# Bias attention and a gated feed-forward on one core: early operations merged, weight conversions moved behind unit 8, a block's last output ahead of a feed-forward step

## Chip, cores, metric

One core of a Trainium2 chip runs the whole program. The metric is the device time of one execution in microseconds. The kernel before took 741.07 us (median of 3 runs, 740.38 to 741.28).

## What is computed

```python
# q, k, v: (4 batches, 8 heads, 576 positions, 64)
scores = scale * np.matmul(q, k.transpose(0, 1, 3, 2))
x = (psi_rel / psi_i)[..., None]          # logs of distances and positions
h = np.maximum(x @ w1 + b1, 0.0)          # 32 hidden values for each pair of positions
bias = h @ w2                             # one value per head, the same for all batches
attn = softmax(scores + bias)
x = np.matmul(attn, v)                    # rows: 2304 tokens of 512
h = x @ w_in                              # 512 -> 2048
out = (h * sigmoid(1.702 * h)) @ w_out    # 2048 -> 512
```

The inputs of the feed-forward part come as 64-bit floats, all others as 32-bit. The softmax is written in the reference with its maximum and its sum.

## The kernel before, in words

**Units.** Attention is cut into 72 units of (batch b, chunk c of 128 query positions, pair of heads hp); a last chunk has 64 positions, and its units take two pairs. Two batches form a group of 36 units. Unit u issues its scores on PE (`emit_s`, L352), then its softmax (`emit_soft1`, L368): DVE adds the bias tile to the scores and finds the extreme (L378, mx), ACT takes the exponential (L385) and sums into sm, ACT or DVE makes an fp16 high part (L392, L390), POOL the low part (hl, L393), and a transposing DMA on SP's queue makes aT (L399). The output of a unit (`emit_av`) follows two units later, three in the first eight: DVE finishes sm (L414) and takes its reciprocal, PE multiplies aT with v16 (L423, L430), DVE writes xn in two fp16 parts (L436, L442). After the last pair of heads SP transposes xn into xT (L452).

**Blocks.** Two batches' outputs of one chunk form a block of 256 tokens (128 for the short chunk). Block 0 is made of units 0 to 7, block 1 of units 8 to 15, and so on. Each block has 16 feed-forward steps. A step's first half (`emit_m1`, L511) is 12 products with xT (L522), tanh on ACT (L528, th), a product on DVE (L530) and two fp16 parts, gT, on DVE or ACT and on POOL (L537, L538). Its second half (`emit_m2`, L541) comes two steps later: PE adds to the block's output in PSUM (L551, tiles op). Behind the 16th step `store` evicts (L561).

**Weights.** Every number of w_in and w_out is a 64-bit float. 32 loads of 512 KB on SP (L467) bring them in, up to three ahead, and `split_w` (L471) converts each: three unpacking instructions on DVE (L486, L489, L492), the high part on ACT (L498), the low part on DVE (`lo_part`, L224). `W_STEPS` (L86) says how many conversions unit u issues; the first half of step f needs the first 8 * (f // 4) + 4 of them.

**Bias.** 36 bias steps make the hidden values on DVE or ACT (L165, L167), multiply on PE (L188, L190), evict on ACT (L195) and store (L196). The first 8 stand before unit 0, the others with units 0 to 28. Steps 1 to 19 use the two PSUM tiles that the feed-forward outputs use later (om and ol).

**Keys and values.** `trans_k`, `trans_k_own` (L273, L286) and `split_v` (L329) transpose the keys on PE and split keys and values into fp16 high (ACT: L282, L296, L305, L344) and low parts (DVE or POOL: L224, L222), one pair of heads at a time.

**Order.** The unit loop (L683) issues, for each unit: scores and softmax, one feed-forward step (if a block is ready), the due outputs, conversions, bias work, another feed-forward step, loads. Each engine then gets a list order from a scheduler that moves instructions by its own estimates, so the lists that the engines run differ somewhat from the order of the source.

Of the kernel before, what the change touches and what calls it, by code (L numbers as in the profile page):

```python
# [20 lines left out]
def kernel(  # L21
# [26 lines left out]
    nc = tc.nc  # L48
# [17 lines left out]

    BUFS = {"st": 4, "ht": 2, "os": 2, "bt": 2, "a32": 2, "hl": 2, "aT": 2, "xT": 2, "w32": 3, "qT": 3, "kT": 8,
            "v16": 8, "gT": 3, "xn": 2}

# [15 lines left out]
    STEPS_B = {}  # L85
    W_STEPS = [1, 2, 2, 3, 3, 3, 3, 3, 3, 3, 3, 3]  # L86

# [4 lines left out]
    ps_h = ctx.enter_context(tc.tile_pool(name="ps_h", bufs=2, space=PSUM))  # L92
    ps_o = ctx.enter_context(tc.tile_pool(name="ps_o", bufs=2, space=PSUM))

# [190 lines left out]

    def trans_k_own(b, e):  # L286

        t = k_st[b, e]
        tails = ps_h.tile([128, 512], F32, tag="h", name="kt")
        ds = []  # L290
        for u in range(2):
            nc.tensor.transpose(tails[:, ST * u:ST * u + ST], kt_st[b][:, 2 * e + u, :], idn[:ST, :ST])
        for u in range(2):
            ds.append(stage([128, 2, S], F16, "kT", "kT"))
            kT[b, 2 * e + u] = ds[u]
            nc.scalar.activation(  # L296
                out=ds[u][:, 0, SM:S], in_=tails[:, ST * u:ST * u + ST], func=ACTF.Copy, scale=KS
            )
        for u in range(2):
            lo_part(False, ds[u][:, 1, SM:S], tails[:, ST * u:ST * u + ST], KS, ds[u][:, 0, SM:S])  # L300
# [28 lines left out]
    def split_v(b, e):  # L329

        src = v_st.pop((b, e)).rearrange("p u c d -> p u (c d)")
        gp = (b, e) in POOL_V
        vs = scaled(gp, src, VS)
        for u in range(2):
            d = stage([128, 2, 640], F16, "v16", "v16")
            nc.gpsimd.memset(d[0:64, :, 320:384], 0.0)
            nc.gpsimd.memset(d[64:128, :, 256:320], 0.0)
            sv, dv = src[:, u], [d[:, x] for x in range(2)]
            parts = [(sv[0:64, 256:320], *(y[0:64, 256:320] for y in dv)),
                     (sv[64:128, 256:320], *(y[64:128, 320:384] for y in dv))]  # L340
            for (x, y) in ((0, 0), (320, 384)):
                parts.append((sv[:, x:x + 256], *(z[:, y:y + 256] for z in dv)))
            for (s_, dh, dl) in parts:
                nc.scalar.activation(out=dh, in_=s_, func=ACTF.Copy, scale=vs)  # L344
                lo_part(gp, dl, s_, vs, dh)
            v16[b, 2 * e + u] = d

# [261 lines left out]
    for g in range(B // 2):  # L609
# [73 lines left out]
    for u in range(NU + 2):  # L683
# [77 lines left out]
```

## Time and profile before

| | |
|---|---|
| runs | 741.07 us median, 740.38 to 741.28 |
| profiled execution | 739.43 us; 737.7 us from first to last instruction |
| PE | 642.0 us busy, 87% |
| DVE | 482.9 us busy, 65% |
| ACT | 406.4 us busy, 55% |
| POOL | 312.2 us busy, 42% |
| granted TensorE clock, mean | 0.955 |
| chain of waits | PE 55%, DMA 18%, DVE 13%, ACT 7% |

PE is busy 9 tenths or more of most slices from 180 us on and 5 to 7 tenths before; DVE and ACT have it the other way round, and the DMA engines are near their full share up to about 180 us. The shares are means over both parts, so the views have to be cut by stage.

### The profile page before, as it was taken

What the parts mean: (1) busy time and instruction counts of PE and PEld (TensorE: products, weight loads), DVE (VectorE), ACT (ScalarE), POOL (GpSimd) and SP (SyncE); (2) the same over time, 40 slices, a digit from 0 to 9 for tenths busy, and PEclk for the clock granted to TensorE, in tenths of its full rate; (3) what the DMA queues carried; (4) which work ended last, traced back from release to release, by engine and by line L of the source; (5) the groups of instructions that cost most, each with busy time, mean ns of one, the idle gap of its engine ahead of it and who ended that gap; (6) DMA issues with size and microseconds to landing.
All of it is one profiled execution on the core that took longest, in us unless ns stands there. A gap on an engine that the chain in (4) does not pass through costs nothing.

```text
span 737.7 us, 17303 instructions
## 1 busy us (share of the span) xinstructions
PE 642.0 (87%) x6648; PEld 400.5 (54%) x6648; DVE 482.9 (65%) x1378; ACT 406.4 (55%) x905; POOL 312.2 (42%) x360
## 2 busy tenths in 40 slices
PE   6767567577989998799979889889989999999997
PEld 3223333344645664566747456566656666667764
DVE  5689698999657766446667676454774777574321
ACT  6899987477457656445445436643443444342133
POOL 2314433246434445444442555643463456453222
PEclk9986798899999999999998999999999999999999
DMA  9799999979767657958576796982794487664000
GB/s 236 231 287 261 236 250 287 273 203 215 177 118 182 157 109 162 170 121 157 129 167 127 146 173 141 183 164 52 130 174 105 97 153 163 111 113 100 9 30 16
DMA packets 249843, 116.50 MB, mean 158 GB/s; under 512 B 229792, under 2 KB 234016, under 8 KB 249760
## 3 DMA queue, kind: packets, MB, share of 16 engines
q1 hardware_dynamic: 241664, 99.38, 65.3%
q10 hardware_dynamic: 7952, 15.43, 6.3%
q8 instruction: 52, 0.85, 0.5%
q0 software_dynamic: 144, 0.59, 0.2%
q14 instruction: 31, 0.25, 0.1%
HBM read 52.85 MB, written 15.34 MB: 92 GB/s over the span
## 4 chain that ended last, share of the span: by engine, by line
PE 55%; DMA 18%; DVE 13%; ACT 7%; issue 4%; POOL 1%; SPq 0%; ACTq 0%; DVEq 0%; POOLq 0%
PE hp L522 21%; PE op L551 19%; DMA aT<-hl 13%; PE ot L430 6%; PE sp L362 4%; DVE a L378 3%; ACT a L385 3%; PE ot L423 2%; DVE w L489 2%; DVE w L492 2%; DMA w<-in_moe_w_in_dram 1%; ACT ht L165 1%; POOL hl L393 1%; PE o L188 1%; DVE w L486 1%
## 5 line engine op out<-in xcount | busy, mean ns | idle before, releaser
L393 POOL TENSOR_TENSOR hl<-a,hl 128x576 f16<-128x576 f32 x142 | 187.8, 1336 | 171.7 <-ACT hl L392 93.2
L522 PE MATMUL hp<-xT,wi 128*128 128x256 f16 (+1 forms) x1920 | 219.1, 265 | 22.4 <-DMA xT<-xn 9.2
L551 PE MATMUL op<-wo,gT 128*128 128x512 f16 x864 | 214.9, 381 | 4.1 <-DVE gT L537 2.6
L522 PEld LDWEIGHTS <-wi 128*128 128x128 f16 x1920 | 169.9, 99 | 65.3 <-issue 29.8
L538 POOL TENSOR_TENSOR gT<-th,gT 128x256 f16<-128x256 f32 (+1 forms) x160 | 106.7, 668 | 206.2 <-DVE gT L537 114.7
L528 ACT ACTIVATE th<-hp 128x256 f32<-128x256 f32 (+1 forms) x160 | 57.2, 359 | 188.7 <-PE hp L522 181.5
L385 ACT ACTIVATE a<-a,mx 128x576 f32<-128x576 f32 x144 | 110.3, 768 | 61.7 <-DVE mx L382 61.4
L530 DVE SCALAR_TENSOR_TENSOR th<-th,hp 128x256 f32<-128x256 f32 (+1 forms) x160 | 62.3, 390 | 105.7 <-ACT th L528 104.7
L378 DVE CUSTOM_DVE_ANT_0 a<-sp,bt 128x576 f32<-128x576 f32 x144 | 102.9, 751 | 29.1 <-PE sp L362 27.9
L551 PEld LDWEIGHTS <-gT 128*128 128x128 f16 x864 | 79.5, 98 | 75.8 <-issue 3.5
L165 ACT ACTIVATE ht<-tab,pk 128x576 f32<-128x576 f32 x96 | 78.6, 866 | 4.2 <-PE ol L190 4.0
L362 PE MATMUL sp<-kT,qT 64*128 64x512 f16 (+2 forms) x960 | 73.1, 296 | 7.3 <-DVE mx L378 6.0
L430 PE MATMUL ot<-v,aT 128*128 128x64 f16 (+1 forms) x1920 | 78.3, 199 | 0.0
L430 PEld LDWEIGHTS <-aT 128*128 128x128 f16 (+1 forms) x1920 | 71.3, 105 | 5.2 <-issue 4.2
L392 ACT CAST hl<-a 128x576 f16<-128x576 f32 x103 | 66.1, 665 | 8.0 <-DMA aT<-hl 7.8
L362 PEld LDWEIGHTS <-qT 64*128 64x128 f16 (+1 forms) x960 | 29.3, 99 | 53.1 <-issue 21.5
L188 PE MATMUL om<-ht,pk 128*32 128x512 f32 x152 | 44.5, 718 | 8.5 <-ACT os L195 8.4
L423 PE MATMUL ot<-v,aT 128*128 128x128 f16 (+1 forms) x240 | 29.2, 231 | 23.2 <-DMA aT<-hl 18.2
L414 DVE TENSOR_SCALAR sm<-sm 128x2 f32<-128x2 f32 x72 | 28.7, 399 | 25.9 <-ACT a L385 25.7
L537 DVE CAST gT<-th 128x256 f16<-128x256 f32 x112 | 42.5, 380 | 4.0
L167 DVE TENSOR_SCALAR ht<-tab,pk,b1n 128x576 f32<-128x576 f32 x48 | 34.4, 763 | 7.8 <-PE o L190 6.0
L423 PEld LDWEIGHTS <-aT 128*128 128x128 f16 (+1 forms) x240 | 17.7, 104 | 38.2 <-DMA aT<-hl 25.5
(65 smaller groups left out, 548.9 us busy)
## 6 DMA issues: line engine op xcount, KB each, us to landing
bt<-scr SPq DMA_DIRECT2D x31, 576.0 KB, 4.6
scr<-os ACTq DMA_DIRECT2D x36, 288.0 KB, 3.9
w<-in_moe_w_in_dram SPq DMA_DIRECT2D x16, 512.0 KB, 5.9
w<-in_moe_w_out_dram SPq DMA_DIRECT2D x16, 512.0 KB, 4.8
k<-in_k_dram SPq DMA_DIRECT2D x32, 128.0 KB, 4.4
q<-in_q_dram SPq DMA_DIRECT2D x16, 256.0 KB, 4.2
out_dram<-ob ACTq DMA_DIRECT2D x16, 256.0 KB, 3.6
bt<-scr SPq DMA_DIRECT2D x8, 288.0 KB, 4.1
```

Of the source, the lines that this page charges most:

```text
L165: nc.scalar.activation(out=h, in_=tv, func=ACTF.Relu, bias=b1c, scale=sc[:, col:col + 1])
L362: nc.tensor.matmul(ps[a][64 * e:64 * e + m, cs], lhsT=qt[r, x, hp + e, 0:m], rhs=kT[b, hp + e][r, y, cs], start=i == 0, stop=i == 2,)
L378: nc.vector.tensor_tensor_reduce(out=at[:, cs], in0=s_ps.pop((u, a))[:, 0:S], in1=bt[:, cs], scale=-1.0 / BS, scalar=3.0e38, op0=ALU.add, ...
L385: nc.scalar.activation(out=at[:, cs], in_=at[:, cs], func=ACTF.Exp, scale=-1.0, bias=mx[:, a:a + 1], accum_out=sm[:, a:a + 1],)
L392: nc.scalar.copy(hl[:, 0, cs], at[:, cs])
L393: (nc.vector if a and u in VEC_EXP_LO else nc.gpsimd).tensor_tensor(out=hl[:, 1, cs], in0=at[:, cs], in1=hl[:, 0, cs], op=ALU.subtract)
L423: nc.tensor.matmul(o[po, 0:128], lhsT=t[:, 9 * y + 4, po], rhs=vt[:, x, 256:384], start=i == 0, stop=False, skip_group_check=True,)
L430: nc.tensor.matmul(o[po, 64 * a:64 * a + 64], lhsT=t[:, 9 * y + 5 * a + kb, po], rhs=vt[:, x, 384 * a + 64 * kb:384 * a + 64 * kb + 64], s ...
L522: nc.tensor.matmul(p[:, :n], lhsT=wi16[:, x, cc, 128 * f:128 * f + 128], rhs=r, start=i == 0, stop=i == 11,)
L530: nc.vector.scalar_tensor_tensor(out=g[:, :n], in0=th[:, :n], scalar=1.0, in1=p[:, :n], op0=ALU.add, op1=ALU.mult)
L538: nc.gpsimd.tensor_tensor(out=gt[:, 1, :n], in0=g[:, :n], in1=gt[:, 0, :n], op=ALU.subtract)
L551: nc.tensor.matmul(op_t[j, i], lhsT=gt[:, x, ts], rhs=wo16[:, f, y, :], start=f == 0 and n3 == 0, stop=f == NF - 1 and n3 == 2,)
```

## The change

1. `W_STEPS`: one conversion for each of units 0 to 7, then four for each of units 8 to 13 (before: 1, 2, 2, then 3 for each of units 3 to 11).
2. A bias step's output is one two-bank PSUM tile with one eviction of 576 columns (before: 512 and 64). The pool `ps_o` has one buffer of two banks instead of two of one; the two feed-forward outputs of a block are its halves.
3. Keys and values: one tile for two pairs of heads (kT and v16 have 4 buffers of twice the size), and one instruction where there were two, but for the transposed halves of `trans_k_own`.
4. A small activation at the head of ACT's list, on a column that nothing else uses yet, with the memset of `oc` moved ahead.
5. sm is a tile of two columns with a gap of one element between them.
6. For blocks 1 to 8, the output of a block's last unit is emitted ahead of the unit's first feed-forward step; for block 0 the second step of unit 9 may already run.

```diff
-            "v16": 8, "gT": 3, "xn": 2}
+            "v16": 4, "gT": 3, "xn": 2}
...
-    W_STEPS = [1, 2, 2, 3, 3, 3, 3, 3, 3, 3, 3, 3]
+    W_STEPS = [1] * 8 + [4] * 6
...
-    ps_o = ctx.enter_context(tc.tile_pool(name="ps_o", bufs=2, space=PSUM))
+    ps_o = ctx.enter_context(tc.tile_pool(name="ps_o", bufs=1, space=PSUM))
...
     def bias_setup():
+        nc.scalar.activation(out=oc[:, 4:5], in_=oc[:, 4:5], func=ACTF.Relu)
...
-            om = ps_o.tile([128, 512], F32, tag="o", name="om")
-            ot = (ps_o if where == "o" else ps_h).tile([128, 512], F32, tag=where, name="ol")[:, 0:ST]
-            outs = [(slice(0, SM), om), (slice(SM, S), ot)]
+            o = ps_o.tile([128, 2, 512], F32, tag="o", name="o").rearrange("p a n -> p (a n)")
+        om, ot = o[:, 0:SM], o[:, SM:S]
...
-        for cs, src in outs:
-            nc.scalar.activation(out=os_[:, cs], in_=src, func=ACTF.Identity, bias=oc[:, na:na + 1])
+        nc.scalar.activation(out=os_, in_=o[:, 0:S], func=ACTF.Identity, bias=oc[:, na:na + 1])
...
-            nc.scalar.activation(out=d[:, 0], in_=ps, func=ACTF.Copy, scale=KS)
-            lo_part(False, d[:, 1], ps, KS, d[:, 0])
+        nc.scalar.activation(out=d[:, :, 0], in_=pair[:, :, 0:S], func=ACTF.Copy, scale=KS)
+        lo_part(False, d[:, :, 1], pair[:, :, 0:S], KS, d[:, :, 0])
...
+        parts = [(slice(0, 64), 256, 256, 64), (slice(64, 128), 256, 320, 64),
+                 (slice(0, 128), 0, 0, 256), (slice(0, 128), 320, 384, 256)]
+        for (po, x, y, n) in parts:
+            s_, (dh, dl) = src[po, :, x:x + n], (d[po, :, z, y:y + n] for z in range(2))
+            nc.scalar.activation(out=dh, in_=s_, func=ACTF.Copy, scale=vs)
+            lo_part(gp, dl, s_, vs, dh)
...
-        sm = wk.tile([128, 2], F32, tag="sm", name="sm", bufs=6)
+        sm = wk.tile([128, 2, 2], F32, tag="sm", name="sm", bufs=6)[:, :, 0]
...
+            t = ps_o.tile([128, 2, 512], F32, tag="o", name="op")
             for i in range(n // 128):
-                op_t[j, i] = ps_o.tile([128, 512], F32, tag="o", name="op")
+                op_t[j, i] = t[:, i]
...
-        msteps(ready, STEPS_A.get(u, 1))
+        late = u - AV_LAG.get(u, 2) in last_unit[1:]
+        if not late:
+            msteps(ready, STEPS_A.get(u, 1))
         while av <= u - AV_LAG.get(u, 2):
             emit_av(av)
             av += 1
+        if late:
+            msteps(ready, STEPS_A.get(u, 1))
+        elif u - 2 == last_unit[0]:
+            ready = NF
```

**Where the lists of the engines move.** ACT behind its first bias work, before (os is a bias step's output in SBUF, ht its hidden values):

```order
L195 ACTIVATE os_153<-o_144,oc_78 128x576
L196 DMA scr0_79<-os_153 128x576
L195 ACTIVATE os_172<-om_162,oc_78 128x512
L195 ACTIVATE os_172<-ol_163,oc_78 128x64
L165 ACTIVATE ht_264<-tab_75,pk_76 128x576
L282 ACTIVATE kT_182<-kp_176 128x576
```

and in the change:

```order
L191 ACTIVATE os_154<-o_145,oc_78 128x576
L192 DMA scr0_79<-os_154 128x576
L191 ACTIVATE os_172<-o_163,oc_78 128x576
L165 ACTIVATE ht_254<-tab_75,pk_76 128x576
L192 DMA scr0_79<-os_172 128x576
L278 ACTIVATE kT_176<-kp_175 128x2x576
```

The second bias step has one eviction in place of two, and the key conversion takes both pairs of heads at once.

DVE between the softmax operations of units 3 and 4, before (w64 is a loaded weight, w32 its unpacking, wo16 the converted weight, a32_833 the softmax of unit 4):

```order
L489 SCALAR_TENSOR_TENSOR w32_766<-w64_748,w32_766 128x512
L382 TENSOR_SCALAR mx_698<-mx_698 128x1 x2
L224 SCALAR_TENSOR_TENSOR wo16_73<-w32_758,wo16_73 128x512
L492 SCALAR_TENSOR_TENSOR w32_766<-w64_748,w32_766 128x512
L486 TENSOR_SCALAR w32_885<-w64_756 128x512
L489 SCALAR_TENSOR_TENSOR w32_885<-w64_756,w32_885 128x512
L492 SCALAR_TENSOR_TENSOR w32_885<-w64_756,w32_885 128x512
L378 ISA a32_833,mx_834<-sp_820,bt_657 128x576
```

and in the change (a32_741 is the softmax of unit 4):

```order
L481 SCALAR_TENSOR_TENSOR w32_898<-w64_676,w32_898 128x512
L371 TENSOR_SCALAR mx_626<-mx_626 128x1 x2
L425 TENSOR_TENSOR xn_641<-ot_645,rv_642 128x128
L431 SCALAR_TENSOR_TENSOR xn_641<-ot_645,rv_642,xn_641 128x64 x2
L406 RECIPROCAL rv_862<-sm_530 128x2
L367 ISA a32_741,mx_742<-sp_728,bt_588 128x576
```

Six conversion instructions stood between the two units, and one does now.

DVE up to the first operation of a feed-forward step (th), before:

```order
L489 SCALAR_TENSOR_TENSOR w32_1434<-w64_1416,w32_1434 128x512
L489 SCALAR_TENSOR_TENSOR w32_1528<-w64_1424,w32_1528 128x512
L492 SCALAR_TENSOR_TENSOR w32_1434<-w64_1416,w32_1434 128x512
L492 SCALAR_TENSOR_TENSOR w32_1528<-w64_1424,w32_1528 128x512
L224 SCALAR_TENSOR_TENSOR wo16_73<-w32_1426,wo16_73 128x512
L530 SCALAR_TENSOR_TENSOR th_1610<-th_1610,hp_1597 128x256
```

and in the change:

```order
L220 SCALAR_TENSOR_TENSOR wi16_72<-w32_1507,wi16_72 128x512
L475 TENSOR_SCALAR w32_1523<-w64_1505 128x512
L220 SCALAR_TENSOR_TENSOR wi16_72<-w32_1515,wi16_72 128x512
L519 SCALAR_TENSOR_TENSOR th_1396<-th_1396,hp_1383 128x256
L519 SCALAR_TENSOR_TENSOR th_1456<-th_1456,hp_1443 128x256
L478 SCALAR_TENSOR_TENSOR w32_1523<-w64_1505,w32_1523 128x512
```

Before, the wo16 operation shown is the 22nd conversion that ends, and one th follows; in the change it is the 19th, and the th of two steps follow.

## Rows read from the trace of the kernel before

**Rows 1.** The windows view by stage, as its first row names the columns.

```profile
core 0: us, PE busy (x) PEld busy (x) DVE busy (x) ACT busy (x) POOL busy (x), PEclk, DMA share, GB/s
0.00:41.00 41.00, 28.65 (x218) 12.99 (x218) 27.11 (x60) 31.77 (x64) 10.04 (x33) 0.96 0.93 241
41.00:119.20 78.20, 51.15 (x455) 23.70 (x457) 66.64 (x166) 70.11 (x140) 27.67 (x25) 0.78 1.00 262
119.20:177.90 58.70, 39.51 (x357) 21.60 (x354) 56.88 (x122) 42.37 (x77) 24.52 (x16) 0.91 0.96 241
177.90:212.50 34.60, 34.21 (x351) 21.01 (x350) 23.34 (x64) 18.77 (x37) 15.32 (x16) 1.00 0.80 166
212.50:680.00 467.50, 436.00 (x4783) 285.12 (x4782) 295.72 (x930) 228.72 (x544) 220.44 (x244) 0.98 0.70 139
680.00:737.70 57.70, 52.50 (x490) 36.04 (x488) 13.22 (x41) 14.63 (x45) 14.22 (x27) 0.99 0.07 20
```

**Rows 2.** DVE's timeline (start us, us): softmax of units 0, 9, 16; first th.

```profile
40.85 0.76 DVE L378 CUSTOM_DVE_ANT_0 a<-sp,bt 128x576 f32<-128x576 f32 x1
...
119.21 0.75 DVE L378 CUSTOM_DVE_ANT_0 a<-sp,bt 128x576 f32<-128x576 f32 x1
...
141.51 0.42 DVE L530 SCALAR_TENSOR_TENSOR th<-th,hp 128x256 f32<-128x256 f32 x1 [0.42 <-ACT th L528]
...
212.48 0.76 DVE L378 CUSTOM_DVE_ANT_0 a<-sp,bt 128x576 f32<-128x576 f32 x1 [0.92 <-PE sp L362]
```

**Rows 3.** The chain that ended last, 60 to 182 us (start us, us).

```profile
123.06 2.00 DVE w L492 x2
...
132.66 1.77 DVE wi L224
```

**Rows 4.** The groups by line: a weight conversion on DVE, then on ACT.

```profile
L486 DVE TENSOR_SCALAR w<-w 128x512 uint32<-128x512 uint32 x32 | 15.7, 494 | 5.3 <-DMA w<-in_moe_w_in_dram 5.1
L489 DVE SCALAR_TENSOR_TENSOR w<-w,w 128x512 uint32<-128x512 uint32 x32 | 22.8, 716 | 0.3
L492 DVE SCALAR_TENSOR_TENSOR w<-w,w 128x512 uint32<-128x512 uint32 x32 | 28.4, 893 | 0.2
L224 DVE SCALAR_TENSOR_TENSOR wi<-w,wi 128x512 f16<-128x512 f32 x16 | 13.8, 866 | 1.4 <-ACT wi L498 1.4
L224 DVE SCALAR_TENSOR_TENSOR wo<-w,wo 128x512 f16<-128x512 f32 x16 | 13.4, 842 | 0.1
L498 ACT ACTIVATE wi<-w 128x512 f16<-128x512 f32 x16 | 10.0, 630 | 6.1 <-DVE w L492 6.1
```

**Rows 5.** The groups by line: the bias evictions on ACT.

```profile
L195 ACT ACTIVATE os<-om,oc 128x512 f32<-128x512 f32 x19 | 12.9, 681 | 1.4 <-PE om L188 0.8 <-PE ol L190 0.4
L195 ACT ACTIVATE os<-ol,oc 128x64 f32<-128x64 f32 x19 | 5.9, 309 | 0.0
L195 ACT ACTIVATE os<-o,oc 128x576 f32<-128x576 f32 x17 | 12.5, 734 | 3.2 <-PE o L190 2.3 <-DMA out_dram<-ob 0.9
```

**Rows 6.** Waits of PE from 180 us on (waiter, releaser: us in total, times, longest).

```profile
PE ot L423 <- DMA aT<-hl: 12.3, 9, 3.0
PE hp L522 <- DMA xT<-xn: 1.7, 2, 1.4
```

**Rows 7.** Waits of DVE from 212.5 us on.

```profile
DVE th L530 <- ACT th L528: 100.8, 91, 4.5
```

**Rows 8.** Durations ns min/median/max by line: sm and mx on DVE, hl on POOL.

```profile
L414 DVE TENSOR_SCALAR sm<-sm x72: 137/169/1266, 46.5 to 670.1; 128x2 f32<-128x2 f32 x72
...
L382 DVE TENSOR_SCALAR mx<-mx x144: 131/147/154, 42.2 to 668.4; 128x1 f32<-128x1 f32 x144
...
L393 POOL TENSOR_TENSOR hl<-a,hl x142: 1269/1282/3194, 46.5 to 671.6; 128x576 f16<-128x576 f32 x142
```

**Rows 9.** The page's part 6: one weight load.

```profile
w<-in_moe_w_in_dram SPq DMA_DIRECT2D x16, 512.0 KB, 5.9
```

**Rows 10.** The groups by line: one eviction of a feed-forward output.

```profile
L561 ACT ACTIVATE ob<-op 128x512 f32<-128x512 f32 x18 | 10.3, 590 | 2.7 <-PE op L551 2.0 <-DMA aT<-hl 0.6
```

More of the change, by code (lines that the diff above doesn't have):

```diff
@@ L65 @@
     WOS = 64.0
-    BUFS = {"st": 4, "ht": 2, "os": 2, "bt": 2, "a32": 2, "hl": 2, "aT": 2, "xT": 2, "w32": 3, "qT": 3, "kT": 8,
-            "v16": 8, "gT": 3, "xn": 2}
+    BUFS = {"st": 4, "ht": 2, "os": 2, "bt": 2, "a32": 2, "hl": 2, "aT": 2, "xT": 2, "w32": 3, "qT": 3, "kT": 4,
+            "v16": 4, "gT": 3, "xn": 2}
     BIAS_ENG = ["VVVA"] * 8 + ["AAAA"] * 16 + ["VVAA"] * 12
@@ L136, in bias_setup @@
         nc.vector.tensor_scalar(out=w2b, in0=w2b, scalar1=BS, scalar2=None, op0=ALU.mult)
-        nc.gpsimd.memset(oc, 0.0)
         p = ps_h.tile([128, 512], F32, tag="h", name="pc")
@@ L176, in bias_products @@
             o = ps_s.tile([128, 4, 512], F32, tag="s", name="o")[:, 0:2].rearrange("p a n -> p (a n)")
-            om, ot = o[:, 0:SM], o[:, SM:S]
-            outs = [(slice(0, S), o[:, 0:S])]
-        else:
-            om = ps_o.tile([128, 512], F32, tag="o", name="om")
-            ot = (ps_o if where == "o" else ps_h).tile([128, 512], F32, tag=where, name="ol")[:, 0:ST]
-            outs = [(slice(0, SM), om), (slice(SM, S), ot)]
+        else:
+            o = ps_o.tile([128, 2, 512], F32, tag="o", name="o").rearrange("p a n -> p (a n)")
+        om, ot = o[:, 0:SM], o[:, SM:S]
         for x in range(2):
@@ L275, in trans_k @@
         pair = ps_s.tile([128, 4, 512], F32, tag="s", name="kp").rearrange("p (u a) n -> p u (a n)", u=2)
+        d = stage([128, 2, 2, S], F16, "kT", "kT")
         for u in range(2):
-            ps, hp = pair[:, u, 0:S], 2 * e + u
             for c in range(4):
-                nc.tensor.transpose(ps[:, 128 * c:128 * c + 128], t[:, u, c, :], idn)
-            nc.tensor.transpose(ps[:, SM:S], kt_st[b][:, hp, :], idn[:ST, :ST])
-            d = stage([128, 2, S], F16, "kT", "kT")
-            nc.scalar.activation(out=d[:, 0], in_=ps, func=ACTF.Copy, scale=KS)
-            lo_part(False, d[:, 1], ps, KS, d[:, 0])
-            kT[b, hp] = d
+                nc.tensor.transpose(pair[:, u, 128 * c:128 * c + 128], t[:, u, c, :], idn)
+            nc.tensor.transpose(pair[:, u, SM:S], kt_st[b][:, 2 * e + u, :], idn[:ST, :ST])
+            kT[b, 2 * e + u] = d[:, u]
+        nc.scalar.activation(out=d[:, :, 0], in_=pair[:, :, 0:S], func=ACTF.Copy, scale=KS)
+        lo_part(False, d[:, :, 1], pair[:, :, 0:S], KS, d[:, :, 0])
     def trans_k_own(b, e):
@@ L289, in trans_k_own @@
         tails = ps_h.tile([128, 512], F32, tag="h", name="kt")
-        ds = []
+        d = stage([128, 2, 2, S], F16, "kT", "kT")
         for u in range(2):
             nc.tensor.transpose(tails[:, ST * u:ST * u + ST], kt_st[b][:, 2 * e + u, :], idn[:ST, :ST])
[L293 to L300, printed above, removed]
+        src = tails[:, 0:2 * ST].rearrange("p (u n) -> p u n", u=2)
+        nc.scalar.activation(out=d[:, :, 0, SM:S], in_=src, func=ACTF.Copy, scale=KS)
+        lo_part(False, d[:, :, 1, SM:S], src, KS, d[:, :, 0, SM:S])
         for u in range(2):
@@ L304, in trans_k_own @@
                 nc.tensor.transpose(ps[:, 128 * c:128 * c + 128], t[:, u, c, :], idn)
-            nc.scalar.activation(out=ds[u][:, 0, 0:SM], in_=ps, func=ACTF.Copy, scale=KS)
-            lo_part(False, ds[u][:, 1, 0:SM], ps, KS, ds[u][:, 0, 0:SM])
+            kT[b, 2 * e + u] = d[:, u]
+            nc.scalar.activation(out=d[:, u, 0, 0:SM], in_=ps, func=ACTF.Copy, scale=KS)
+            lo_part(False, d[:, u, 1, 0:SM], ps, KS, d[:, u, 0, 0:SM])
     def load_v(b, e, tag="st"):
@@ L333, in split_v @@
         vs = scaled(gp, src, VS)
-        for u in range(2):
[L335 to L346, printed above, removed]
+        d = stage([128, 2, 2, 640], F16, "v16", "v16")
+        nc.gpsimd.memset(d[0:64, :, :, 320:384], 0.0)
+        nc.gpsimd.memset(d[64:128, :, :, 256:320], 0.0)
+        parts = [(slice(0, 64), 256, 256, 64), (slice(64, 128), 256, 320, 64),
[4 more added lines that the diff above has]
+            lo_part(gp, dl, s_, vs, dh)
+        for u in range(2):
+            v16[b, 2 * e + u] = d[:, u]
     s_ps, a_t, rs_t, aT = {}, {}, {}, {}
@@ L628 @@
                 at(o + u, *x)
+    nc.gpsimd.memset(oc, 0.0)
     nc.sync.dma_start(out=tab, in_=dist.rearrange("p (f a) -> p f a", a=LPH))
```

## Prediction

> **What bounds the kernel now.** I read the windows view first, cut where the character of the program changes [rows 1], then DVE's timeline for the times of the cuts [rows 2], then the chain of waits [rows 3], then the groups by line for the price of each operation [rows 4, 5, 10], and last the waits of PE and DVE in the late part [rows 6, 7].
>
> The reader is to see three stages in [rows 1]. Up to 41 us, when unit 0's softmax starts [rows 2], ACT leads: 31.8 us busy, while DVE has 27.1. From 41 to 119.2 us (units 0 to 8) PE works 51.2 of 78.2 us, ACT 70.1, DVE 66.6, and the DMA share is 1.00: three resources are nearly full, and PE isn't one of them. From 119.2 to 177.9 DVE works 56.9 of 58.7 us, PE 39.5: DVE is the bound, and the chain of waits there runs through weight conversions [rows 3]. Then it turns: 34.2 of 34.6 us for PE up to unit 16 at 212.5, 436.0 of 467.5 up to 680, 52.5 of 57.7 to the end. So what happens before unit 16 decides when PE becomes the bound, and after it time can only come out of PE's 31.5 + 5.2 us of idle time.
>
> The first feed-forward step reaches DVE (the first th) only at 141.5 us [rows 2]. By the order, 22 of 32 conversions stand ahead of it on DVE. One conversion costs DVE (15.7 + 22.8 + 28.4 + 13.8 + 13.4) / 32 = 2.94 us and ACT 0.63 us [rows 4].
>
> **Why unit 16 is the place to compare.** Counted in the order of both kernels, exactly the same stands on PE ahead of unit 16's scores: 15 output units of attention, 15 first halves and 14 second halves of feed-forward steps, the same bias products. On DVE the same stands ahead of its softmax but for 4 + 8 key and value operations that are merged away. So if unit 16 comes x us earlier, the rest of the program is x us earlier, as long as its own waits stay.
>
> **The change, part by part.**
>
> Merged operations on ACT. [Rows 5] price one: 681 + 309 against 734 ns, 256 ns less for one instruction that goes. An end of one may lie under the start of the next, so I take 0.2 us, and 0.13 and 0.26 as ends. Ahead of unit 0's exponential the order has 20 such instructions fewer (9 evictions, 3 kT, 8 v16): 4.0 us (2.6 to 5.1). ACT leads there, so I put all of it on the path: unit 0 at 37 us. The small activation at the start, which draws the table load ahead of the pack's arrival, lies in the same stretch; I count it at nothing, since the first evictions wait for DVE and PE anyway, and its uncovered end would be a little more gain.
>
> Conversions moved. Ahead of unit 9's softmax the order has 9 unpacking instructions fewer on DVE (51 to 42) and 4 subtractions fewer (16 to 12): 9 x 0.70 + 4 x 0.85 = 9.7 us. On ACT it has 18 more merged instructions gone (3.6 us) and 3 conversions fewer (3 x 0.63 = 1.9 us), together 5.5 us. On SP, 14 weight loads instead of 20 stand ahead of the first xT transpose, so fewer transposes queue behind a load that waits for its buffer; 4 loads of 512 KB [rows 9] at 262 GB/s are 8 us of a full DMA. The least of the three savings holds, ACT's 5.5 us, with ACT's 8.1 us of idle time kept: units 0 to 8 take 72.7 instead of 78.2 us, and unit 9 starts at 119.2 - 4.0 - 5.5 = 109.7. The ends are 0 (the stage goes by latencies that stay) and 9.7 us (DVE goes alone).
>
> The conversions come back between units 9 and 16: DVE's 80.2 us of work there become 80.2 + 9.7 = 89.9. With the idle share of the DVE-bound stretch today, 1.8 of 58.7 us or 3%, that is 92.7 us, and unit 16 starts at 109.7 + 92.7 = 202.4 instead of 212.5. PE's work in it, 39.5 + 34.2 = 73.7 us, is the same and fits under it. Ends: 89.9 us (no idle time), or 103.0 us (today's 13.1 us of idle time all stay), which leaves nothing of the gain. The cover of the moved conversions is thus PE's wait for DVE that exists already; what they take away is DVE's slack from 177.9 on.
>
> The sm tile with a gap between its two columns. [Rows 8] show sm at 137 to 1266 ns, the one-column mx never above 154, and POOL's hl at 1282: sm waits for a running POOL instruction. If the gap ended that, up to 16 x 0.25 us (mean 399 against 146) or 4 us would go ahead of unit 16. The Trainium skill (SBUF — State Buffer, Who interferes with whom) says that a DVE operation in a two-port mode and a GpSimd instruction block each other for a whole instruction, and its page VectorE: DVE Perf Modes (Mode 2×_2P) asks only for an even outermost count, not for neighbouring elements. Two columns with a gap are still two, so by it nothing is saved; the trace agrees on the blocking (1266 against 1282 ns) and can't show the gap's effect. I take 0, and keep 4 us for the range.
>
> Late in the program. The last output unit of a block now stands ahead of a feed-forward step on PE, so its xn operations on DVE and its xT transpose on SP start up to one step earlier. PE's waits for xT from 180 us on sum to 1.7 us [rows 6], so 1 us is to be had. Against it, the output's own aT transpose has one step less time; such waits cost PE 12.3 us in 9 cases, 3.0 at most [rows 6]. The feed-forward outputs share one two-bank tile, so a new block waits for both evictions of the old: 9 times at most 0.59 us [rows 10], mostly under the first step of the new block. I put these at 0 together, with -1 and +8 x 3.0 + 5.3 = 29 us as far ends, of which a few us are likely.
>
> Sum: 4.0 + 5.5 + (93.3 - 92.7) = 10.1 us. The profiled execution took 739.43 us (737.7 of span), so 729.3; the median of the runs, 741.07, is 1.6 above it. **Forecast 731 us**, its own range 727 to 737.
>
> **The rivals.**
>
> More than that. DVE runs units 9 to 16 without idle time (+2.8), units 0 to 8 shrink by DVE's 9.7 (+4.2), and sm no longer waits (+4): 10.1 + 11 = 21 us, 720 at the far end. For it: 34.6 - 23.3 us of DVE's idle time fall away by construction. Against it: ACT was busy 90% of units 0 to 8.
>
> Given back. Unit 16 comes early, but the units behind it meet the same transposes and evictions with less time: five boundaries with 2 us each, and the end is at 741, no change. For it: PE already waits for aT. Against it: the stretch up to 680 has the same DVE and ACT work, at 63% and 49% busy.
>
> Slower: DVE is held up in order. In the crowded units 9 to 16, a th operation at the head of DVE's queue waits for ACT's tanh and PE's products, while the conversions that are now the bound stand behind it. Where DVE isn't the bound, it waits 100.8 us in 91 cases for them, 1.1 us each [rows 7]; 15 such waits are 16.5 us, and unit 16 would come at 109.7 + 92.7 + 16.5 = 218.9: 6 us late, 747. It decides from 0.7 us a wait on, where the 10 us are used up. Against it: of the first steps today one waited 0.42 us [rows 2], since DVE ran late against its suppliers.
>
> That the change doesn't do what it says can be left out for the conversions: the order shows them moved.
>
> **How the numbers follow.** 0.2% is 1.5 us, about what a measurement of this kernel tells from no change: 739.6 to 742.6 is the same. Forecast 0.55, more 0.13, given back 0.17, slower 0.15. Of the given-back cases half end under 739.6: faster 0.55 + 0.13 + 0.09 = 0.77, same 0.08, slower 0.15. The range takes in the forecast's own, nearly all of the larger gain down to 721, the given-back cases and the slower ones up to 745; about 0.15 lies outside.
>
> **What would show it.** In the changed profile: unit 0's softmax near 37 us, unit 9's near 110, the first th near 129 (unit 9 plus the 22.3 us of today less one conversion), unit 16's near 202; DVE over 95% busy from unit 9 to the last conversion, which ends near unit 15; from unit 16 on the same PE idle time, about 37 us. The forecast is wrong if unit 9 isn't at least 6 us early (the ACT price or the cover), if DVE has more than 10 us of idle time between units 9 and 16 (held up in order), or if PE's idle time behind unit 16 grows by over 5 us (given back).

## The result and the profile after

The changed kernel took 733.07 us (median of 8 runs, 727.13 to 737.49) against 741.17 us (8 runs, 737.96 to 745.70): a ratio of 0.9889, 95% interval 0.9852 to 0.9926. Eleven more runs of the same kernel gave 734.90 against 740.55, 0.9916 (0.9883 to 0.9949). So it is 6 to 8 us faster, and 731 was forecast. But the profile after doesn't show it where the forecast put it.

The windows view of the changed kernel, cut at the same times as [rows 1]:

```profile
core 0: us, PE busy (x) PEld busy (x) DVE busy (x) ACT busy (x) POOL busy (x), PEclk, DMA share, GB/s
0.00:41.00 41.00, 24.70 (x218) 11.37 (x219) 26.45 (x54) 30.05 (x46) 8.14 (x21) 0.96 0.96 247
41.00:119.20 78.20, 50.85 (x447) 21.16 (x446) 57.56 (x148) 61.35 (x110) 26.93 (x21) 0.78 0.97 235
119.20:177.90 58.70, 46.17 (x437) 24.98 (x437) 56.66 (x127) 46.47 (x85) 24.60 (x18) 0.88 0.93 239
177.90:212.50 34.60, 28.44 (x290) 16.20 (x281) 31.83 (x74) 20.55 (x40) 15.55 (x14) 1.00 0.85 216
212.50:680.00 467.50, 438.66 (x4798) 286.23 (x4799) 295.07 (x909) 225.74 (x524) 220.90 (x237) 0.98 0.69 140
680.00:737.70 57.70, 50.30 (x477) 34.95 (x474) 12.43 (x39) 14.57 (x45) 13.48 (x26) 0.96 0.06 17
```

DVE's timeline of the changed kernel (start us, us), the rows that answer to [rows 2]:

```profile
40.77 0.76 DVE L367 CUSTOM_DVE_ANT_0 a<-sp,bt 128x576 f32<-128x576 f32 x1 [3.91 <-DMA bt<-scr]
...
119.17 0.75 DVE L367 CUSTOM_DVE_ANT_0 a<-sp,bt 128x576 f32<-128x576 f32 x1
...
139.95 0.74 DVE L519 SCALAR_TENSOR_TENSOR th<-th,hp 128x256 f32<-128x256 f32 x2
...
211.48 0.76 DVE L367 CUSTOM_DVE_ANT_0 a<-sp,bt 128x576 f32<-128x576 f32 x1
```

From 41 to 119.2 us ACT has 8.8 us less to do and DVE 9.1 us less, as the change promised, and yet unit 0 starts at 40.8, unit 9 at 119.2 and unit 16 at 211.5: 0.1, 0.0 and 1.0 us earlier. The relief became idle time. DVE's work came back from 177.9 us on (31.8 of 34.6 us, 23.3 before), as the moved conversions had to. What is new is the wait in the first row: DVE stands 3.9 us ahead of unit 0 for its bias tile. The profiled execution took 737.28 us, 4 us above its median, so this trace holds 2.2 of the 6 to 8 us.

Two chains end at unit 0. The bias tile comes by the eighth bias eviction on ACT, its store, and a load on POOL's queue; the scores on PE wait for the keys. PE's scores of unit 0 and POOL's load of the tile, before:

```profile
39.31 0.91 PE L362 MATMUL sp<-kT,qT 64*128 64x512 f16 x12 [0.21 <-DVE kT L224]
...
34.27 0.75 POOL L210 DMA_DIRECT2D bt<-scr  x1 [5.89 <-DVE kT L224]
```

and in the changed kernel:

```profile
29.70 0.91 PE L351 MATMUL sp<-kT,qT 64*128 64x512 f16 x12 [1.88 <-DVE kT L220]
...
33.81 0.75 POOL L206 DMA_DIRECT2D bt<-scr  x1 [6.82 <-ACT kT L296]
```

The scores came 9.6 us earlier. The load is issued 0.5 us earlier and takes 6.9 instead of 6.4 us to land, so the tile is there at 40.7 in both. Before, DVE had other work up to 40.7, so no wait gave the second chain away.

The merges didn't bring the tile's chain forward. The eighth eviction ends at 30.3 us in the changed kernel and ended at 29.6 before, since ACT's list now has key conversions ahead of it. ACT's timeline before:

```profile
29.32 0.32 ACT L195 ACTIVATE os<-ol,oc 128x64 f32<-128x64 f32 x1
...
32.79 0.65 ACT L282 ACTIVATE kT<-kp 128x576 f16<-128x576 f32 x1 [1.63 <-PE kp L280]
```

and in the changed kernel:

```profile
27.14 1.11 ACT L278 ACTIVATE kT<-kp 128x1152 f16<-128x1152 f32 x1
...
29.55 0.75 ACT L191 ACTIVATE os<-o,oc 128x576 f32<-128x576 f32 x1
```

### The profile page after: what moved, and what is told of

It reads as the page before. It is cut to its first block, busy times and chain, and to the rows that moved or that the text cites. A ratio compares the mean times of both kernels' runs of the same rounds, so it can differ in the third digit from the quotient of the medians.

```text
span 735.5 us, 17200 instructions
## 1 busy us (share of the span) xinstructions
PE 639.1 (87%) x6648; PEld 394.9 (54%) x6648; DVE 480.0 (65%) x1346; ACT 398.7 (54%) x847; POOL 309.6 (42%) x336
## 4 chain that ended last, share of the span: by engine, by line
PE 51%; DMA 17%; DVE 14%; ACT 9%; issue 5%; POOL 2%; SPq 1%; ACTq 0%; another core or an unknown queue 0%; POOLq 0%; DVEq 0%
PE hp L511 19%; PE op L541 17%; DMA aT<-hl 13%; PE ot L419 5%; PE sp L351 4%; DVE a L367 3%; ACT a L374 3%; ACT ht L165 2%; PE ot L412 2%; DMA xT<-xn 2%; DVE w L478 2%; PE o L185 1%; ACT hl L381 1%; DVE w L481 1%; DVE w L475 1%
## 5 line engine op out<-in xcount | busy, mean ns | idle before, releaser
L382 POOL TENSOR_TENSOR hl<-a,hl 128x576 f16<-128x576 f32 x142 | 190.0, 1352 | 157.8 <-ACT hl L381 73.6
L165 ACT ACTIVATE ht<-tab,pk 128x576 f32<-128x576 f32 x96 | 78.3, 862 | 16.8 <-PE o L187 11.3
L351 PE MATMUL sp<-kT,qT 64*128 64x512 f16 (+1 forms) x960 | 73.0, 297 | 15.1 <-DVE mx L367 9.8
L185 PE MATMUL o<-ht,pk 128*32 128x512 f32 x288 | 66.9, 679 | 11.1 <-ACT os L191 7.1
L419 PEld LDWEIGHTS <-aT 128*128 128x128 f16 (+1 forms) x1920 | 70.4, 104 | 7.6 <-issue 6.2
L381 ACT CAST hl<-a 128x576 f16<-128x576 f32 x103 | 66.4, 664 | 14.0 <-DMA aT<-hl 13.5
L403 DVE TENSOR_SCALAR sm<-sm 128x2 f32<-128x2 f32 x72 | 31.5, 437 | 31.4 <-ACT a L374 31.1
L425 DVE TENSOR_TENSOR xn<-ot,rv 128x128 f16<-128x128 f32 x72 | 20.6, 287 | 40.0 <-PE ot L419 39.0
L412 PEld LDWEIGHTS <-aT 128*128 128x128 f16 (+1 forms) x240 | 17.0, 101 | 52.9 <-DMA aT<-hl 38.1
```

The lines of the kernel that those rows point to most:

```text
L165: nc.scalar.activation(out=h, in_=tv, func=ACTF.Relu, bias=b1c, scale=sc[:, col:col + 1])
L185: nc.tensor.matmul(om[po], lhsT=w2b, rhs=h[:, :, 0:128], start=True, stop=True)
L351: nc.tensor.matmul(ps[a][64 * e:64 * e + m, cs], lhsT=qt[r, x, hp + e, 0:m], rhs=kT[b, hp + e][r, y, cs], start=i == 0, stop=i == 2,)
L381: nc.scalar.copy(hl[:, 0, cs], at[:, cs])
L382: (nc.vector if a and u in VEC_EXP_LO else nc.gpsimd).tensor_tensor(out=hl[:, 1, cs], in0=at[:, cs], in1=hl[:, 0, cs], op=ALU.subtract)
L419: nc.tensor.matmul(o[po, 64 * a:64 * a + 64], lhsT=t[:, 9 * y + 5 * a + kb, po], rhs=vt[:, x, 384 * a + 64 * kb:384 * a + 64 * kb + 64], s ...
```

## Experiments

A row per kernel of the main readings; the starts, DVE's idle time between units 9 and 16, and the span are of the profiled execution, in us. The ratio is the recorded one of all runs, with its interval; it isn't quite the ratio of the two medians.

| kernel | unit 0 | unit 9 | unit 16 | DVE idle 9 to 16 | span | ratio to before (95%) |
|---|---|---|---|---|---|---|
| before | 40.9 | 119.2 | 212.5 | 13.1 | 737.7 | 1 |
| changed | 40.8 | 119.2 | 211.5 | 4.8 | 735.5 | 0.9889 (0.9852 to 0.9926) |
| a1_again | 40.3 | 122.0 | 214.5 | 4.1 | 735.4 | 0.9916 (0.9883 to 0.9949) |
| a2_oldsteps | 41.0 | 118.5 | 216.0 | 18.3 | 731.5 | 0.9954 (0.9925 to 0.9982) |
| a3_notlate | 40.3 | 119.3 | 217.5 | 13.2 | 739.4 | 0.9967 (0.9936 to 0.9999) |
| a4_steps | 42.9 | 119.5 | 209.1 | 3.9 | 737.5 | 0.9991 (0.9963 to 1.0019) |
| b1_freebias | 32.7 | 110.9 | 198.6 | 5.2 | 722.0 | 0.9709 (0.9651 to 0.9768) |
| b2_noconv | 44.7 | 115.7 | 206.0 | 4.8 | 734.5 | 0.9965 (0.9935 to 0.9995) |
| b3_merges | 41.6 | 119.8 | 209.9 | 11.3 | 734.5 | 1.0002 (0.9973 to 1.0031) |
| c1_halfloads | 40.2 | 111.8 | 208.6 | 16.4 | 730.2 | 0.9926 (0.9887 to 0.9965) |
| d3_beforefree | 45.1 | 122.8 | 208.9 | 9.2 | 736.1 | 0.9985 (0.9957 to 1.0014) |
| d4_order | 42.6 | 115.2 | 210.7 | 8.1 | 740.8 | 0.9963 (0.9939 to 0.9988) |
| d5_both | 47.3 | 119.9 | 218.9 | 16.3 | 736.7 | 0.9975 (0.9947 to 1.0002) |
| d9_bothchains | 32.5 | 111.0 | 214.7 | 21.4 | 733.6 | 0.9920 (0.9888 to 0.9952) |

**The changed kernel again, and its parts.** a1_again is the changed kernel without an edit.

> The changed kernel once more, for a second trace: in the first one units 0, 9 and 16 start at 40.8, 119.2 and 211.5 us, against 40.9, 119.2 and 212.5 before, so the gain stands in none of the places where the forecast put it. Forecast's theory (relief of ACT and DVE ahead of unit 16): that trace was an odd one, and in a run near the median of 733 us unit 9 starts at 110 to 114 and unit 16 at 202 to 206. Rival L (the early part gives nothing, the gain lies behind unit 16): unit 0 within 1 us of 40.8, unit 9 within 2 us of 119.2, unit 16 within 3 us of 211.5 whatever the run's time. Rival C (the granted clock makes the run's time): starts as under L, and the time goes with the mean granted clock, some 4 us for 0.005.

Rival L's starts held but for unit 9, 2.8 us late, with unit 16 (214.5) at the edge of its 3 us: a second trace has no early gain either. But neither trace is of a run near the median, so where a run of 731 us gains its time stays open. Rival C fell as a rule for single runs: this trace has a granted clock of 0.961, the first one 0.950, and both took 737.2 us.

a2_oldsteps:

```diff
-    W_STEPS = [1] * 8 + [4] * 6
+    W_STEPS = [1, 2, 2, 3, 3, 3, 3, 3, 3, 3, 3, 3]
```

> The changed kernel with the old W_STEPS (conversions early). Forecast's theory: the 5.5 us of units 0 to 8 go, 733 becomes 738 to 739, unit 9 starts 5 us later than in the changed kernel. Rival L (units 0 to 8 go by the transposes of aT and not by DVE or ACT): unit 9 within 2 us of 119, unit 16 within 3 us of 211.5, the time within 2 us of 733; it may even be faster, since DVE has 7 us less work between units 9 and 16.

a3_notlate:

```diff
-        late = u - AV_LAG.get(u, 2) in last_unit[1:]
-        if not late:
-            msteps(ready, STEPS_A.get(u, 1))
+        msteps(ready, STEPS_A.get(u, 1))
...
-        if late:
-            msteps(ready, STEPS_A.get(u, 1))
-        elif u - 2 == last_unit[0]:
-            ready = NF
```

> The changed kernel with a block's last output emitted behind the feed-forward step again, and no second step of block 0 in unit 9. Forecast's theory counted this part at 0 (between -1 and a few us of loss): 732 to 734. Rival L: this part is the gain, and the time goes back to 738 to 741, with PE's idle time behind unit 16 up by 4 us or more; unit 16 unchanged within 3 us.

a4_steps is the kernel before with the change's `W_STEPS`:

> The kernel before with the new W_STEPS alone. Forecast's theory: the relief of units 0 to 8 by 5.5 us, 741 becomes 735 to 736, unit 9 at 114. Rival L: 741 within 2 us, or slower by up to 4 us as DVE's work moves into units 9 to 16 for nothing; unit 9 within 2 us of 119.

b3_merges has the edits of a2_oldsteps and a3_notlate together:

> The changed kernel with the old W_STEPS and the old place of a block's last output: what is left are the merged operations, the two-bank output tile, the activation at the start and the gap in sm. Forecast's theory: the merges alone are worth 4.0 us at unit 0 and up to 3.6 behind it, so 733 to 737. Theory D (the merges take no byte from the DMA engines): within 2 us of 740.5, unit 16 at 211 to 217. If the parts simply add up (late output 3.7, conversions 2.7 of a gain of 6.2 us by the means of the runs so far): 740.

Of these four only a4_steps went as one side, Rival L, had it (739.08, unit 9 at 119.5). a2_oldsteps (736.05) lies between the two, and its unit 16 came 4.5 us later than in the changed kernel. a3_notlate (737.99) is slower than the forecast's 732 to 734, but its unit 16 came 6.0 us later and PE's idle time behind it, 32.3 us, didn't grow (34.4 in the changed kernel), so Rival L didn't hold either. b3_merges (738.78) is slower than the forecast's 733 to 737; theory D's time fits it, but not D's place for unit 16 (209.9, where 211 to 217 was expected).

By the ratios, the merges with what goes with them are worth nothing (1.0002). On top of them W_STEPS brings 0.35% (a3_notlate), the late output 0.48% (a2_oldsteps); the sum, 0.83%, is near the 0.84 to 1.11% of the whole. So some 2.6 us come from the conversions and 3.5 from the late output, each with about 3 us of uncertainty, so that the part of W_STEPS is not clear of nothing. The medians alone read 1.4 and 3.3 us, and 1.2 for the merges. Alone on the kernel before W_STEPS brings nothing measurable. Unit 16 scatters from 209 to 217 us in these traces, and not in the order of the times.

**The two chains at unit 0.** b1_freebias (the steps 6 and 7 also leave the buffers of the tile):

```diff
+            src = dist if u < 2 else scr[c][:, hh:hh + 2, :].rearrange("p h n -> p (h n)")
-            (nc.sync if u else nc.gpsimd).dma_start(out=t[po, :], in_=scr[c]...
+            (nc.sync if u else nc.gpsimd).dma_start(out=t[po, :], in_=src)
```

> The changed kernel in which the bias tiles of units 0 and 1 (which units 2 and 3 share) are loaded from the table of distances, of the same size, and so wait for no bias step; the output of those units is not the reference's. In the five traces so far unit 0 starts at 40.3 to 42.9 us, and in the changed kernel its scores end at 30.6 and its softmax waits 3.9 us for the bias tile. If unit 0 is bound by the chain eviction, store, load: unit 0's softmax starts at 31 to 37 us. If it is bound by ACT (the forecast): no earlier than 39. Theory D (the DMA engines are the bound up to unit 16: share times time is 197 to 204 us there in every trace): the head start is lost, unit 16 stays at 210 to 217 and the time at 731 to 737. Theory L (a chain of latencies from unit to unit): it is kept, unit 9 at 113 to 117, and the time falls by 3 to 6 us.

d3_beforefree is the same edit on the kernel before:

> The kernel before with the bias tiles of units 0 and 1 loaded from the table of distances, as in b1_freebias (the output of the units that use them is not the reference's). In the changed kernel that brought unit 0 from 40.8 to 32.7 us, unit 9 to 110.9, unit 16 to 198.6, and the time from 734 to 718. Theory B (the bias tile of unit 0, and not ACT, bound the start in the kernel before too, so that the merges had nothing to save there): unit 0 at 32 to 37 us, and the time at 724 to 733. The forecast's theory (ACT leads up to unit 0, with 4.0 us more to do than in the changed kernel): unit 0 no earlier than 39, the time within 3 us of 740.

The windows view of b1_freebias, units 0 to 8, 9 to 15 and the rest (columns as above):

```profile
32.66:110.85 78.19, 50.40 (x485) 21.08 (x485) 67.05 (x163) 70.83 (x125) 28.50 (x21) 0.83 1.06 263
110.85:198.58 87.73, 74.81 (x712) 42.08 (x712) 82.49 (x191) 64.01 (x120) 36.24 (x31) 0.94 0.94 239
198.58:722.00 523.42, 490.25 (x5271) 320.48 (x5270) 310.70 (x950) 240.63 (x569) 234.61 (x264) 0.98 0.62 127
```

The timelines of PE and DVE up to unit 0 in d3_beforefree:

```profile
39.08 0.61 PE L363 MATMUL sp<-kT,qT 64*128 64x512 f16 x2 [0.37 <-DVE kT L225]
...
43.33 0.43 DVE L487 TENSOR_SCALAR w<-w 128x512 uint32<-128x512 uint32 x1 [2.24 <-DMA w<-in_moe_w_in_dram]
...
45.12 0.75 DVE L379 CUSTOM_DVE_ANT_0 a<-sp,bt 128x576 f32<-128x576 f32 x1
```

With the tile free, the changed kernel starts unit 0 8.1 us earlier, and all of it stays: 8.3 at unit 9, 12.9 at unit 16, 13.5 in the span, some 15 by the medians (718.43). That is more than any of the theories had. The 4.6 us won between units 9 and 16 are not explained, and there are only four runs, 712.24 to 723.73 us, of which the profiled one is the slowest. The kernel before gains nothing from the same edit (739.41 against 741.15), since its scores are issued at 39.1 and a conversion that waits 2.2 us for its load stands ahead of the softmax. Theory B fell for the kernel before. The forecast's numbers held in this run (unit 0 not before 39, the time within 3 us of 740), but in b1_freebias its 39 us fell, with unit 0 at 32.7, so it isn't ACT that holds unit 0. Each chain hides the other. The change shortens the one of the scores (0.8 to 1.1% in all, none of it ahead of unit 9), the free tile the other (0.15%, within its interval); the two together give 2.9%.

**What units 0 to 8 go by.** b2_noconv has `W_STEPS = [0] * 8 + [4] * 8`; c1_halfloads:

```diff
-        t = stage([128, 512, 2], U32, "st", "w64")
+        t = stage([128, 256, 2], U32, "st", "w64")
...
-        lo, hi = t[:, :, 0], t[:, :, 1]
+        lo, hi = (t[:, :, x].unsqueeze(1).to_broadcast([128, 2, 256]) for x in range(2))
```

> The changed kernel with no conversion in units 0 to 7 and four for each of units 8 to 15: 8 conversions and their loads, that is 23.5 us of DVE, 5 us of ACT and 4 MB (16 us at 262 GB/s), leave units 0 to 8. Forecast's theory (ACT is the least of the savings there): unit 9 4 to 6 us earlier, at 114 to 117. Theory D: unit 9 12 to 16 us earlier, at 104 to 109. Theory L: unit 9 within 2 us of 119 to 122. Behind it DVE has about 111 us of work up to unit 16, so under all of them units 9 to 16 take at least 111 us and the whole is slower than the changed kernel unless unit 9 comes 18 us earlier.

> The changed kernel with weight loads of half the size (256 KB; each conversion reads its half twice, so the operations on DVE and ACT stay and the second half of the weights is not the reference's): 8 MB less, some 32 us of DMA time at 262 GB/s. Theory D: unit 16 comes 15 to 30 us earlier, at 185 to 200 (DVE's 145 us of work between units 0 and 16 is the next bound, at 186), and the time falls by at least 10 us. Theory L: unit 16 within 4 us of 211 to 215. Forecast's theory (DMA's 8 us was counted as a saving of its own beside ACT's and DVE's): unit 9 no more than 2 us earlier, since ACT is the least.

In b2_noconv the scheduler drew conversions forward, 32 unpacking instructions between units 0 and 9 against 33 in the changed kernel, so the run doesn't take their work out of the stretch, and my 111 us for units 9 to 16 were wrong too (90.4). Unit 9, at 115.7, lies in the forecast's range, but unit 0 came 3.9 us late: the stretch took 7.4 us less with as many unpackings. c1_halfloads brings unit 9 7.4 us forward with 39 of them, where the forecast had at most 2. The windows view of units 0 to 8 in the changed kernel, b2_noconv and c1_halfloads:

```profile
40.77:119.17 78.40, 50.82 (x447) 21.16 (x446) 57.76 (x148) 61.55 (x110) 26.93 (x21) 0.78 0.97 236
...
44.66:115.66 71.00, 49.42 (x448) 19.25 (x444) 56.64 (x143) 58.92 (x105) 23.34 (x16) 0.81 0.90 228
...
40.16:111.76 71.60, 48.15 (x454) 20.76 (x453) 65.11 (x154) 62.58 (x111) 29.23 (x21) 0.80 0.90 206
```

The two shorter ones move fewer bytes: GB/s times us gives 16.2 and 14.7 MB against 18.5. Over all 14 traces, the four stretches with 14.7 to 17.7 MB (these two, d4_order and d5_both below) took 71.0 to 72.6 us, the ten with 18.5 to 20.5 MB took 76.6 to 81.7. DVE's work doesn't sort them: b1_freebias takes 78.2 us with 43 unpacking instructions, the changed kernel 78.4 with 33. So transfers, more than the conversions' work, set that stretch, at least in part; by which wait isn't shown, and each run has lists of its own. The transposes of aT alone aren't it. PE's waits for them between units 0 and 9 (us in total, times, longest), before, in the changed kernel and in a2_oldsteps:

```profile
PE ot L423 <- DMA aT<-hl: 5.7, 2, 4.5
...
PE ot L412 <- DMA aT<-hl: 12.2, 4, 4.3
...
PE ot L412 <- DMA aT<-hl: 0.5, 1, 0.5
```

The stretches took 78.4, 78.4 and 77.5 us. Theory D fell all the same: in c1_halfloads unit 16 came only 2.9 us earlier and the time not at all (732.94), as DVE then idles 16.4 us between units 9 and 16.

**A version with both chains shortened.** d4_order (st7 is the store of the eighth bias step):

```diff
+    first = ExitStack()
+    first.enter_context(tc.issue_after(st7.ins))
     for x in SECOND:
...
+        if u == 1:
+            first.close()
```

> The changed kernel with what ACT has behind the eight bias steps in the source (v16, the keys of the second batch, the second query tile's conversion, conversions) also behind their last store in ACT's list; output as the reference's. In the changed kernel the eighth bias eviction stands at 29.55 us, behind 8 v16 and 3 kT operations, its store lands at 33.7 and the tile at 40.7. Theory B: the eighth eviction at 24 to 26, the tile and unit 0 at 35 to 38, and most of that kept: 726 to 731 us. Rival (units 0 to 3 wait for v16 and kT instead): unit 0 at 35 to 38, but unit 4 no earlier than 66, and 732 to 737 us.

d5_both adds (unit 0's tile is allocated ahead of the bias steps, and the store stays for the other units):

```diff
+        if c == 0:
+            for e in range(2):
+                nc.gpsimd.dma_start(out=bt_t[0][16 * s:16 * s + 16, S * e:S * e + S], in_=os_[e:128:8])
```

> The order of d4_order, and unit 0's bias tile written straight from the eviction tiles in SBUF, 16 positions and one head in each of 16 small transfers on POOL's queue, in place of the store and a load from DRAM; output as the reference's. Theory B: the tile is complete 3 to 5 us behind the eighth eviction, at 28 to 31, and unit 0 starts when its scores allow, at 31 to 35; the time 717 to 726 us, as in b1_freebias. Rival (the 16 transfers hold POOL, or wait in the full DMA queues, so that the tile is no earlier than in d4_order): unit 0 at 35 to 39 and the time within 2 us of d4_order.

In d4_order the tile's load is issued at 29.59, 4.2 us earlier, but DVE and PE read:

```profile
37.13 0.43 DVE L477 TENSOR_SCALAR w<-w 128x512 uint32<-128x512 uint32 x1 [6.88 <-DMA w<-in_moe_w_in_dram]
...
38.87 0.61 PE L353 MATMUL sp<-kT,qT 64*128 64x512 f16 x2 [4.26 <-DVE kT L222]
```

The keys of the second batch stand behind a conversion whose load, on SP, stands behind unit 1's bias tile. The scores became the late chain again, and in d5_both more so (42.2). Unit 0, at 42.6 and 47.3 us, came later than either side had it in both, and the times (736.92 and 738.63) are above the changed kernel's.

d9_bothchains keeps the direct writes of d5_both and those keys ahead, and puts conversions and v16 behind unit 0 on DVE:

```diff
+        if u == 0:
+            first.enter_context(tc.issue_after(soft[0].ins))
+            split_v(0, 0)
...
-            (nc.sync if u else nc.gpsimd).dma_start(out=t[po, :], ...
+            (nc.sync if u > 1 else nc.gpsimd).dma_start(out=t[po, :], ...
```

> The changed kernel with both chains to unit 0 shortened, output as the reference's: v16's operations and the conversions stand behind the eighth bias step on ACT and behind unit 0's softmax on DVE, while the keys of the second batch stay ahead; unit 0's bias tile is written straight from the eviction tiles (as in d5_both), unit 1's is loaded on POOL's queue, so that SP's weight loads queue behind neither; a third buffer for the eviction tiles. In d4_order and d5_both the tile came at about 35 and 33 us, but unit 0's scores stood behind keys that stood behind a weight conversion (scores at 38.9 and 42.2). Theory T (two chains, the bias tile and the scores, meet at unit 0; only shortening both helps, and what is won there stays): scores end by 31, unit 0 at 30 to 34, unit 9 at 109 to 114, the time at 716 to 727 us. Rival (the conversions that now start behind unit 0, and the weight loads that wait for v16's tiles, give it back): unit 0 at 30 to 34, but unit 9 at 117 or later and 732 to 738 us.

Its scores start at 26.9 us, unit 0 at 32.5, unit 9 at 111.0, as theory T said. But units 9 to 16 took 103.7 us, and the time is 735.34 against 740.10, like the changed kernel's: the rival's time, though not by its unit 9 (117 or later). The windows view of that stretch in d9_bothchains:

```profile
111.00:214.68 103.68, 78.76 (x738) 43.76 (x739) 82.23 (x200) 64.06 (x117) 37.42 (x30) 0.86 0.94 232
```

and its waits of PE (us in total, times, longest), the largest:

```profile
PE ot L418 <- DMA aT<-hl: 19.8, 6, 6.5
```

DVE idles 21.4 us: PE waits 19.8 us for aT transposes, one of them 6.5, where b1_freebias has 2.4 us in this stretch. So no version with the whole computation beats the changed kernel here, and what is won at unit 0 need not stay. b1_freebias, which leaves out the bias of four units, is the one run in which it did; how much of its 15 us a whole kernel could keep isn't shown.

## Why the prediction was right in size, and not by its steps

- *"ACT leads there, so I put all of it on the path: unit 0 at 37 us."* This step failed. The price of a merge was right: two keys cost ACT 1122 ns against 2 x 648, two halves of v16 622 against 2 x 410, an eviction 731 against 681 + 309, so 0.17 to 0.26 us each. The groups by line, before:

```profile
L344 ACT ACTIVATE v<-v 128x256 f16<-128x256 f32 x32 | 11.9, 410 | 2.5 <-PE ot L430 2.2
...
L282 ACT ACTIVATE kT<-kp 128x576 f16<-128x576 f32 x12 | 7.8, 648 | 10.2 <-PE kp L280 10.2
```

  and in the changed kernel:

```profile
L191 ACT ACTIVATE os<-o,oc 128x576 f32<-128x576 f32 x36 | 26.3, 731 | 5.3 <-PE o L187 3.3 <-DMA out_dram<-ob 1.5 <-ACT os L191 0.4
...
L332 ACT ACTIVATE v<-v 128x512 f16<-128x512 f32 x16 | 9.4, 622 | 1.1 <-DMA scr<-os 0.6 <-ACT a L374 0.4
...
L278 ACT ACTIVATE kT<-kp 128x1152 f16<-128x1152 f32 x6 | 6.7, 1122 | 5.1 <-PE kp L276 5.0
```

  The path was wrong: just ahead of unit 0 DVE was busy and showed no wait, and I took ACT's busy share for the chain, without asking when the tile itself landed (34.27 + 6.4 us). In all, 7.6 of the forecast's 10.1 us were merged instructions on ACT (4.0 and 3.6), and b3_merges, which has them without the other two parts, gains nothing within some 2 us.
- *"The least of the three savings holds, ACT's 5.5 us."* This failed too, at its lower end of 0. ACT's busy time between units 0 and 9 fell by 8.7 us, DVE's by 9.0, and the stretch stayed at 78.4 (81.7 in the second trace). In its place, as above, transfers seem to set the stretch.
- *Units 9 to 16 in 92.7 us, DVE over 95% busy, the last conversion near unit 15.* This held: 92.3 and 92.6 us in the two traces. The windows view up to the last conversion's end at 202.76 (unit 15 starts at 202.7):

```profile
119.17:202.76 83.59, 67.95 (x641) 37.46 (x637) 81.48 (x182) 61.25 (x113) 36.27 (x28) 0.92 0.88 230
```

  That is 97%; DVE waited 0.4 us for a tanh in one case, so the slower rival had no ground. Started at 119 instead of 110, the stretch ends where the old one did; the first th, forecast at 129, came at 139.95.
- *The gap in sm: 0.* This held. The Trainium skill (VectorE: DVE Perf Modes, Mode 2×_2P) asks for an even outermost count there. Two columns with a gap are still two, and the trace agrees: sm went on waiting, with 437 ns on average against 399, the longest 1295 against 1266 [rows 8].

```profile
L403 DVE TENSOR_SCALAR sm<-sm x72: 154/170/1295, 47.7 to 667.4; 128x2 f32<-128x2 f32 x72
```

- *The late output: 0.* This was mis-sized: by the ratios it brings about 3.5 us. PE's waits for xT, where the text had 1 us to be had, rose; its place isn't shown. PE's waits from 180 us on in the changed kernel, the rows that answer to [rows 6]:

```profile
PE ot L412 <- DMA aT<-hl: 15.8, 10, 4.3
...
PE hp L511 <- DMA xT<-xn: 4.9, 2, 3.8
```

  Both are 3 us more than before (12.3 and 1.7), as the text feared of aT, within its far ends.
- *What is gained at unit 16 stays.* Seen once, and not shown as a rule: b1_freebias, 12.9 us at unit 16 and 13.5 in the span. Against it, b2_noconv reached unit 16 5.5 us ahead of the changed kernel and its span is 1.0 us shorter, and a2_oldsteps reached it 4.5 us behind and its span is 4.0 us shorter. Both kernels have the same 5271 matmuls from unit 16 on; they take 525.2 us before, 524.0 and 520.9 in the changed kernel's two traces. What is gained at unit 9 doesn't stay by itself: by unit 16 c1_halfloads had lost 4.5 of its 7.4 us and d9_bothchains all of its 8.2.

So the number came out by luck: 731 lies 2 to 4 us from the medians, while the text's own test (unit 9 at least 6 us early) says that the forecast was wrong in its reason. Two terms of 9.5 us weren't there. The late output, put at 0, and W_STEPS, whose gain was put in units 0 to 8, brought some 6 by the ratios. The rival that the gain is given back at the blocks isn't seen either: PE's idle time behind unit 16 is 34.4 us against 36.7 before. Open is by which waits W_STEPS and the late output earn their 2.6 and 3.5 us: both profiled executions of the changed kernel were near the top of their range (737.28 and 737.24), and the places scatter between lists by more than that. There is a hint for the late output: from unit 16 to the end the nine traces that have it take 522.3 us on average (515.6 to 530.1), the five without it 525.5 (521.9 to 528.4). The difference has the right size, but each set scatters by more.

## What to carry to other kernels

Ahead of a place where engines meet, list when every input of the waiting instruction arrives, transfers too; an engine that is busy up to the moment hides a second chain that ends with the first. Savings on engines that are 85% busy are bounds, not gains, when transfers stand between them. And where a scheduler draws up the lists, test a mechanism by where the program's marks stand in the trace, and a part's worth by the runs: the two can disagree.

## What was not expected of the hardware

The same list of the changed kernel took 727.13 to 738.14 us in 19 runs, with a granted TensorE clock of 0.947 to 0.965 on average over the run (1 is 2.4 GHz). In the first eight runs 0.01 of it went with 4.6 us, though not in every run. PE's busy share alone doesn't tell the clock: in the first trace it is 0.96 up to 41 us, where PE works 24.7 us, 0.78 from there to 119.2 us, where PE works 50.9 of 78.2, and 0.98 from 212.5 to 680 us, where it works 94%. In a2_oldsteps' trace the stretch behind unit 16 took 515.5 us at a granted clock of 0.99 with PE busy 482.7, against 524.0 at 0.98 with 489.7 in the changed kernel's first trace. A single profiled execution thus can't settle a difference below 1%.
